# V sums of a block moved ahead of the next K block's last score set, or ahead of its maxima

## The chip, the cores and the metric

The kernel runs on one core of a Trainium2 chip. The metric is the device time of one execution in microseconds. Three executions of the kernel before took 405.64, 403.96 and 405.98 us; the median is 405.64 us.

## The reference

One token of decoding. The input row is normalised, and then an attention block over a cached context and a mixer MLP are both applied to the normalised row and added to it. Cut to what matters:

```python
# x: 1 x 1024 (bf16), 32 query heads, 4 KV heads, 65536 cached keys, head size 128
xn = layernorm(x)
q = (xn @ wq)                                     # 32 heads of 128
scores = einsum("bhqd,bhkd->bhqk", q, k) * (128 ** -0.5)   # 8 query heads share one KV head
o = einsum("bhqk,bhkd->bhqd", softmax(scores), v)
attention = o @ wo
h = gelu(layernorm(xn) @ w1)
x1 = xn + shifted(h) @ w2      # S = 1: the shift along the sequence brings in zeros
mlp = x1 + gelu(layernorm(x1) @ w3) @ w4
out = xn + attention + mlp
```

The K and V caches are 4 x 65536 x 128 bf16 each, 67 MB apiece. With the weights, 169.87 MB are read from HBM in each execution.

## The kernel before, in words

**Blocks and slots.** Each KV head's cache is cut into two blocks of 32768 keys. There are eight K blocks, K0 to K7, and eight V blocks, V0 to V7; each is one transfer of 128 partitions x 32768 bf16, 8.39 MB. On-chip memory has room for three such tiles, `slot0`, `slot1` and `slot2`. The table `home` (lines 285 to 288) says who lives where: even K blocks in slot 0, odd K blocks in slot 2, V0 to V6 in slot 1, V7 in slot 0. The weights pass through the same slots: wq in 0, w3 and later wo in 1, w1 and w2 and later w4 in 2.

**Transfers.** All large loads are issued by SP, one after the other, in the order in which they are recorded: wq, w3, w1 and w2, K0, K1, V0, K2, and then by the list `stream` (line 524): after the V sums of block u come V(u+1) and K(u+3); after block 5 come V6 and V7, after block 6 wo and w4 in five pieces. A load waits on SP until the readers of its slot are done; what is queued behind it waits too.

**The recorder.** Nothing is emitted directly. A `Program` records every operation with the regions of memory that it reads and writes, in the order of the Python code. `plan` (line 124) then goes through the list and gives each operation the waits that this order implies: an operation that reads or writes a region waits for the earlier operations that wrote it, and one that writes a region also for the earlier ones that read it. Each engine executes its operations in the recorded order. In the profile almost all operations therefore have one of the recorder's lines (82, 89, 102, 106, 116, 122), and they are told apart by their tiles.

**One block u.** `scores(u)` (line 453) handles the K block in four sets (`SETS`), each a quarter of every partition's words. For a set, DVE transposes the quarter in place (tile `slot`), and PE then runs 16 matmuls of it against the placed queries (`qdiag`) into `sc`. All 64 matmuls of a block accumulate into the same four PSUM banks. `maxima(u)` (line 469) takes the maximum of `sc` on DVE into `mx`, turns it with a small PE matmul into `pm`, reduces and scales it there, turns it back, and copies it to `nball`. `weights(u)` (line 480) makes `p_sb` with one Exp on ACT, and DVE transposes `p_sb`. `values(u, after)` (line 486) runs 64 matmuls of `p_sb` against the V block into `oacc`, and then records the loads in `after`, here `stream[u]`. `first_rows` copies `oacc` to `og` on ACT after the first block of a head; `group_weights` and `group_rows` bring both blocks of a head together on DVE, with one PE matmul.

**The loop.** Block 0 goes through scores, maxima and weights first. Then for u from 0 to 6 the loop records the scores of block u+1, its maxima, on odd u the group weights, the V sums of block u, the rows, and the weights of block u+1. There is one `p_sb`, so the weights of block u+1 can be written only when the V sums of block u have read theirs.

**The end.** After the last V sums, PE adds o @ wo and the last MLP product as the pieces of wo and w4 land, and the result is stored.

Of the kernel before, what the change touches and what calls it, by code (L numbers as in the profile page):

```python
# [17 lines left out]
SETS = 4  # L18
# [188 lines left out]
def kernel(  # L207
# [83 lines left out]
    def load(it):  # L291
        t = tiles[it]
        if it == "wq":
            prog.load("sp", t[:], A_wq.rearrange("(p c) n -> p (c n)", c=DC))
        elif it == "w3":
            prog.load("sp", t[:, 0:DC * F], B_w3.rearrange("(p c) f -> p (c f)", c=DC))
        elif it == "w12":
            prog.load("sp", t[:, 0:DC * D], B_w1.rearrange("(p c) n -> p (c n)", c=DC))
            prog.load("sp", t[:, DC * D:2 * DC * D], B_w2.rearrange("(m c) n -> m (c n)", c=DC))
        elif it == "wo":  # L300
            prog.load("sp", t[:], A_wo.rearrange("(p j) n -> p (j n)", p=P))
        elif it == "w4":
            w4_v = B_w4.rearrange("(m c) n -> m c n", c=FC)
            c0 = 0
            for n in W4_PIECES:
                prog.load("sp", t[:, c0 * D:(c0 + n) * D], w4_v[:, c0:c0 + n, :].rearrange("p c n -> p (c n)"))
                c0 += n
        else:
            kind, i = it
            g, b = divmod(i, NB)  # L310
            cache = A_k_cache if kind == "K" else A_v_cache
            prog.load("sp", t[:], cache[0, g, b * UKEYS:(b + 1) * UKEYS, :].rearrange("(p ct) d -> p (ct d)", p=P))
# [96 lines left out]
    def place_queries(g):  # L409
        for a in range(4):  # L410
            at = slice(32 * a, 32 * a + 32)
            pool.tensor_copy(
                out=qdiag[at, LEAD:].rearrange("p (x c) -> p x c", x=4)[:, :, 32 * a:32 * a + 8],
                in_=qx[at, :, 8 * g:8 * g + 8])
# [35 lines left out]
    rl = sb("rl", [P, 1])  # L450
    o5 = sb("o5", [P, 32])

    def scores(u):
        g, b = divmod(u, NB)
        if b == 0:
            place_queries(g)
        t = tiles["K", u]
        cols = t[:].rearrange("p (s u k b x r) -> p s u k b x r", u=SUBS, s=SETS, k=16, b=2, r=2)
        for s in range(SETS):
            words = t[:, W * s:W * (s + 1)].bitcast(F32)  # L460
            dve.transpose(out=words, in_=words)
            for b2 in range(2):
                for r in range(2):
                    c0 = LEAD + P * (2 * b2 + r) - 8 * s
                    for e in range(SUBS):
                        pe.mm(sc[:, e, :], qdiag[:, c0:c0 + P], cols[:, s, e, :, b2, :, r],
                              s == 0 and b2 == 0 and r == 0, s == SETS - 1 and b2 == 1 and r == 1)

    def maxima(u):
        g, b = divmod(u, NB)  # L470
        dve.reduce_max(out=mx[:], in_=sc[:].rearrange("p e n -> p (e n)"), axis=AX.X)
        at = next_pm()
        pe.turn32(at[0:1, 0:P], mx[:, 0:1], ident_f[:])
        dve.tensor_reduce(out=m8[:], in_=at[0:1, 0:P].rearrange("o (j h) -> o h j", h=8), axis=AX.X, op=ALU.max)
        dve.tensor_scalar(out=rep[:].rearrange("o (j h) -> o j h", h=8),
                          in0=m8[:].unsqueeze(1).to_broadcast([1, P // 8, 8]), scalar1=-SCALE, scalar2=None, op0=ALU.mult)
        pe.turn32(at[:, P:P + 1], rep[0:1, :], ident_f[0:1, 0:1])
        dve.tensor_copy(out=nball[g % 2][:, b:b + 1], in_=at[:, P:P + 1])

    def weights(u):  # L480
        g, b = divmod(u, NB)
        act.activation(out=p_sb[:], in_=sc[:].rearrange("p e n -> p (e n)"), func=ACTF.Exp,
                       bias=nball[g % 2][:, b:b + 1], scale=SCALE, accum_out=lall[g % 2][:, b:b + 1])
        dve.transpose(out=p_sb[:], in_=p_sb[:])

    def values(u, after):
        vt = tiles["V", u][:].rearrange("p (s u t d) -> p s u t d", u=SUBS, s=SETS, t=16)
        for e in range(SUBS):
            for t in range(16):
                q = t % 4  # L490
                pe.mm(oacc[32 * q:32 * (q + 1), :], p_sb[:, 512 * e + 32 * t:512 * e + 32 * (t + 1)],
                      vt[:, :, e, t, :], e == 0 and t < 4, e == SUBS - 1 and t >= 12, (0, 32 * q), COLS)
        for it in after:
            load(it)

    def first_rows():
        act.copy(out=og[:], in_=oacc[:])

    def group_weights(g):
        dve.tensor_reduce(out=negmg[:], in_=nball[g % 2][:], axis=AX.X, op=ALU.min)  # L500
        act.activation(out=wb[:], in_=nball[g % 2][:], func=ACTF.Exp, bias=negmg[:, 0:1], scale=-1.0)
        dve.tensor_scalar(out=og[:], in0=og[:], scalar1=wb[:, 0:1], scalar2=None, op0=ALU.mult)
        dve.tensor_tensor_reduce(out=lw[:], in0=lall[g % 2][:], in1=wb[:], scale=1.0, scalar=0.0,
                                 op0=ALU.mult, op1=ALU.add, accum_out=ol[:, DH:DH + 1])

    def group_rows(g):
        at = next_pm()
        dve.scalar_tensor_tensor(out=og[:], in0=oacc[:], scalar=wb[:, 1:2], in1=og[:], op0=ALU.mult, op1=ALU.add)
        own = og[:].rearrange("p (s d) -> p s d", d=DH)
        dve.tensor_tensor(out=own, in0=own, in1=mask4[:].unsqueeze(2).to_broadcast([P, 4, DH]), op=ALU.mult)  # L510
        dve.tensor_reduce(out=ol[:, 0:DH], in_=og[:].rearrange("p (s d) -> p d s", d=DH), axis=AX.X, op=ALU.add)
        pe.mm32(at[:, 0:DH + 1], selx[:], ol[:], True, True)
        mine = slice(32 * g, 32 * g + 32)
        dve.reciprocal(out=rl[mine, :], in_=at[mine, P:P + 1])
        dve.tensor_tensor(out=msk[mine, :].rearrange("p (q j) -> p q j", q=4),
                          in0=at[mine, 0:P].rearrange("p (q j) -> p q j", q=4),
                          in1=maskq[mine, :].unsqueeze(2).to_broadcast([32, 4, 32]), op=ALU.mult)
        dve.tensor_reduce(out=o5[mine, :], in_=msk[mine, :].rearrange("p (q j) -> p j q", q=4), axis=AX.X, op=ALU.add)
        dve.tensor_scalar(out=oT[mine, :], in0=o5[mine, :], scalar1=rl[mine, 0:1], scalar2=None, op0=ALU.mult)
# [3 lines left out]
    compute_w12()  # L523
    stream = [[("V", u + 1), ("K", u + 3)] for u in range(NU - 3)] + [[("V", NU - 2), ("V", NU - 1)], ["wo", "w4"]]
    scores(0)
    load(("K", 2))
    maxima(0)
    weights(0)
    for u in range(NU - 1):
        g, b = divmod(u, NB)  # L530
        scores(u + 1)
        maxima(u + 1)
        if b == 1:
            group_weights(g)
        values(u, stream[u])
        if b == 0:
            first_rows()
        else:
            group_rows(g)
        weights(u + 1)  # L540
# [81 lines left out]
```

## Time and profile before

| What | Value |
|---|---|
| median of 3 runs | 405.64 us (403.96 to 405.98) |
| profiled execution, its own time | 404.04 us |
| its span, first to last instruction | 402.6 us |
| mean granted TensorE clock | 0.792 |
| PE busy | 221.1 us (55%) |
| DVE busy | 209.9 us (52%) |
| ACT busy | 27.2 us (7%) |
| HBM read | 169.87 MB, mean 422 GB/s over the span |
| SP's transfers | 98.1% of 16 engines' span |

How to read the rows that follow: times are microseconds from the first instruction. "PE", "DVE", "ACT" and "POOL" are TensorE, VectorE, ScalarE and GpSimd; "SPq" is a transfer's issue on SyncE, not its duration. "slot<-slot" is DVE's transpose of a quarter of a K block, "sc<-slot,qdiag" a score matmul, "oacc<-slot,p_sb" a matmul of the V sums. PEclk is the TensorE clock that was granted, as a share of full speed. The DMA share is the mean busy share of the core's 16 DMA engines.

### The profile page before, as it was taken

To read this page: it belongs to the slowest core of one execution; us is meant where nothing else is said; L and a number is where in the kernel's file an instruction comes from. 1 tells how busy PE (TensorE), PEld (TensorE's weight loads), DVE (VectorE), ACT (ScalarE), POOL (GpSimd) and SP (SyncE) were. 2 spreads that over 40 slices of the span, in tenths; PEclk is the share of its full clock that TensorE was granted. 3 is DMA by queue.
4 is the path that set the end of the run, shared out by engine and by line. 5 is a ranking of instruction groups with operands and counts; after the bars stand their busy time and mean duration, and the time that the engine had idled before them with its cause. 6 is when DMAs were issued, how large, how long until landed. Compare 5 with 4: busy or idle time off the path is not lost.

```text
span 402.6 us, 2557 instructions
## 1 busy us (share of the span) xinstructions
PE 221.1 (55%) x1360; PEld 46.2 (11%) x890; DVE 209.9 (52%) x156; ACT 27.2 (7%) x35; POOL 6.2 (2%) x29
## 2 busy tenths in 40 slices
PE   0250970591794497369607850976096329625096
PEld 0210010000001012101200020002011101112043
DVE  0520010966963983696249647950795669322101
ACT  1010030002002000200020020002000200020000
POOL 2000000000000000000000000000000000000000
PEclk9996896696699597659667985696589859987579
DMA  9989999999997999999999999999999999999995
GB/s 365 462 371 430 457 417 449 463 430 423 423 417 314 417 469 464 417 417 417 425 417 443 482 412 417 423 430 417 488 425 417 423 430 423 484 423 418 394 440 242
DMA packets 3760, 170.03 MB, mean 422 GB/s; under 512 B 419, under 2 KB 421, under 8 KB 678
## 3 DMA queue, kind: packets, MB, share of 16 engines
q1 hardware_dynamic: 3744, 169.87, 98.1%
q8 instruction: 9, 0.15, 0.1%
q14 instruction: 1, 0.01, 0.0%
q10 hardware_dynamic: 6, 0.00, 0.0%
HBM read 169.87 MB, written 0.00 MB: 422 GB/s over the span
## 4 chain that ended last, share of the span: by engine, by line
DMA 49%; PE 25%; DVE 23%; ACT 1%; SPq 1%; issue 1%
DMA slot<-in_A_k_cache_dram 33%; PE sc L106 16%; DVE slot L82 16%; DMA slot<-in_B_w_dram 11%; PE oacc L106 7%; DMA slot<-in_A_wq_dram 5%; DVE mx L82 3%; DVE p_sb L82 2%; ACT p_sb L82 1%; PE pm L122 1%; SPq L89 1%; DVE m L82 0%; DVE og L82 0%; DVE rep L82 0%; DVE ol L82 0%
## 5 line engine op out<-in xcount | busy, mean ns | idle before, releaser
L106 PE MATMUL sc<-slot,qdiag 128*128 128x512 bf16 x512 | 130.7, 417 | 91.2 <-DVE slot L82 91.0
L82 DVE STREAM_TRANSPOSE slot<-slot 128x4096 f32<-128x4096 f32 x32 | 139.2, 4408 | 27.1 <-DMA slot<-in_A_k_cache_dram 27.1
L82 DVE STREAM_TRANSPOSE p_sb<-p_sb 128x2048 bf16<-128x2048 bf16 (+2 forms) x10 | 20.8, 2083 | 55.9 <-ACT p_sb L82 55.7
L106 PE MATMUL oacc<-slot,p_sb 128*32 128x512 bf16 x512 | 42.5, 506 | 8.9 <-DMA slot<-in_A_v_cache_dram 8.9
L102 PEld LDWEIGHTS <-qdiag 128*128 128x128 bf16 x128 | 13.3, 104 | 204.1 <-issue 204.1
L82 DVE TENSOR_REDUCE mx<-sc 128x1 f32<-128x2048 f32 x8 | 18.3, 2292 | 30.1 <-PE sc L106 30.1
L106 PE MATMUL sc<-slot,ln_rep_b 128*32 128x512 bf16 (+1 forms) x80 | 16.3, 834 | 9.7 <-DMA slot<-in_B_w_dram 9.5
L102 PEld LDWEIGHTS <-p_sb 128*32 128x32 bf16 x512 | 16.6, 123 | 31.5 <-issue 20.6
L82 ACT ACTIVATE p_sb<-sc,nball 128x2048 bf16<-128x2048 f32 x8 | 15.8, 1970 | 49.6 <-DVE nball L82 36.0
L106 PE MATMUL psB<-slot,oT 128*32 128x512 bf16 x64 | 9.3, 461 | 11.0 <-DMA slot<-in_A_wo_dram 11.0
L82 DVE SCALAR_TENSOR_TENSOR og<-oacc,wb,og 128x512 f32<-128x512 f32 x4 | 3.0, 751 | 20.1 <-PE oacc L106 20.1
L82 DVE TENSOR_TENSOR og<-psB,slot 64x512 f32<-64x512 f32 x1 | 0.7, 684 | 24.2 <-PE psB L106 24.2
L122 PE MATMUL pm<-ident_f,mx 128*1 128x128 f32 x8 | 2.4, 295 | 19.1 <-DVE mx L82 19.1
L82 ACT COPY og<-oacc 128x512 f32<-128x512 f32 x4 | 2.3, 586 | 142.8 <-PE oacc L106 142.8
L116 PE MATMUL pm<-ol,selx 128*128 128x129 f32 x8 | 2.6, 414 | 10.6 <-DVE ol L82 10.6
L116 PE MATMUL pm<-ln_rowsum_a,msk 128*128 128x1 f32 x2 | 0.6, 363 | 13.4 <-DVE ln_rowsum_a L82 13.4
L106 PE MATMUL sc<-slot,ln_rep_a 128*32 128x512 bf16 x64 | 5.1, 488 | 4.7 <-DMA slot<-in_A_wq_dram 4.7
L82 POOL COPY qdiag<-qx 32x32 bf16<-32x32 bf16 x16 | 3.2, 203 | 261.5 <-PE sc L106 235.4
L82 ACT ACTIVATE wb<-nball,negmg 128x2 f32<-128x2 f32 x4 | 1.2, 296 | 89.6 <-DVE negmg L82 89.6
L82 DVE STREAM_TRANSPOSE p_sb<-x_row 32x256 bf16<-32x256 bf16 x4 | 2.5, 616 | 7.5 <-DMA x_row<-in_A_x_dram 7.5
L102 PEld LDWEIGHTS <-oT 128*32 128x32 bf16 x64 | 4.2, 113 | 15.7 <-issue 12.3
L106 PE MATMUL psB<-slot,hT 128*32 128x512 bf16 x40 | 4.7, 379 | 1.2 <-DMA slot<-in_B_w_dram 1.2
(86 smaller groups left out, 61.2 us busy)
## 6 DMA issues: line engine op xcount, KB each, us to landing
slot<-in_B_w_dram SPq DMA_DIRECT2D x1, 7168.0 KB, 37.7
slot<-in_B_w_dram SPq DMA_DIRECT2D x3, 2048.0 KB, 43.2
slot<-in_B_w_dram SPq DMA_DIRECT2D x1, 3072.0 KB, 39.5
slot<-in_B_w_dram SPq DMA_DIRECT2D x1, 1280.0 KB, 42.1
slot<-in_B_w_dram SPq DMA_DIRECT2D x1, 512.0 KB, 42.9
slot<-in_B_w_dram SPq DMA_DIRECT2D x1, 256.0 KB, 43.0
slot<-in_A_k_cache_dram SPq DMA_DIRECT2D x8, 43.6
slot<-in_A_v_cache_dram SPq DMA_DIRECT2D x8, 27.8
```

The costliest lines, as they stand in the source:

```text
L82: return program.add(Op(engine, lambda: method(*args, **kw), reads, writes, alone=kw.get("accum_out") is not None))
L89: return self.add(Op(engine, lambda: e.dma_start(out=out, in_=in_), [], [out], transfer=True))
L102: self.add(Op("pe", lambda: pe.ldweights(lhsT, tile_position=pos), [lhsT], []))
L106: return pe.add_instruction(mybir.InstMatmult(name=nc.get_next_instruction_name(), engine=mybir.EngineType.PE, start_tensor_calc=start, st ...
L116: return self.add(Op("pe", lambda: pe.matmul(out, lhsT=lhsT, rhs=rhs, start=start, stop=stop, tile_position=pos, skip_group_check=True), [ ...
L122: return self.add(Op("pe", lambda: pe.transpose(out, in_, identity), [in_, identity], [out]))
```

## The change

The function `scores` takes a callable, `before_last`, and runs it ahead of its last set. For u = 0 the loop passes in the V sums of block 0 with their loads; they are then recorded between the third and the fourth set of block 1. For u from 1 to 6 the V sums with their loads are recorded after the scores of block u+1 and ahead of its maxima. All other steps keep their order. The number of instructions on each engine stays the same.

```diff
-    def scores(u):
+    def scores(u, before_last=lambda: None):
         g, b = divmod(u, NB)
         if b == 0:
             place_queries(g)
         t = tiles["K", u]
         cols = t[:].rearrange("p (s u k b x r) -> p s u k b x r", u=SUBS, s=SETS, k=16, b=2, r=2)
         for s in range(SETS):
+            if s == SETS - 1:
+                before_last()
             words = t[:, W * s:W * (s + 1)].bitcast(F32)
             dve.transpose(out=words, in_=words)
...
     for u in range(NU - 1):
         g, b = divmod(u, NB)
-        scores(u + 1)
+        if u == 0:
+            scores(1, lambda: values(0, stream[0]))
+        else:
+            scores(u + 1)
+            values(u, stream[u])
         maxima(u + 1)
         if b == 1:
             group_weights(g)
-        values(u, stream[u])
         if b == 0:
             first_rows()
         else:
```

## The prediction

> **What bounds the kernel now.** I read the page first, its slices above all, then the stretches by time, the issues on SP's queue, and the chain of waits.
>
> The slices of the page (busy tenths of the DMA engines, GB/s):
>
> ```profile
> span 402.6 us, 2557 instructions
> DMA  9989999999997999999999999999999999999995
> GB/s 365 462 371 430 457 417 449 463 430 423 423 417 314 417 469 464 417 417 417 425 417 443 482 412 417 423 430 417 488 425 417 423 430 423 484 423 418 394 440 242
> ```
>
> The transfers fill the whole span but for one slice, the thirteenth (120.8 to 130.8 us): 7 tenths, 314 GB/s. By stretches (the last two columns are DMA share and GB/s, the one before them PE's clock):
>
> ```profile
> 110.00:120.00 10.00, 9.71 (x46) 0.96 (x10) 6.57 (x2) 0.00 (x0) 0.00 (x0) 1.00 0.98 426
> 120.00:131.00 11.00, 4.31 (x68) 1.91 (x67) 4.00 (x5) 2.55 (x3) 0.81 (x4) 1.00 0.74 293
> 131.00:170.00 39.00, 24.50 (x132) 4.67 (x84) 27.70 (x22) 2.35 (x3) 0.00 (x0) 0.73 1.00 431
> 170.00:209.00 39.00, 23.53 (x130) 4.20 (x82) 22.68 (x11) 2.55 (x3) 0.81 (x4) 0.72 1.01 431
> ```
>
> Outside 120 to 131 us the DMA engines are full at about 431 GB/s while PE and DVE each idle for over a quarter of the time. SP's issues say why the hole is there:
>
> ```profile
> 91.13 0.33 SPq L89 DMA_DIRECT2D slot<-in_A_k_cache_dram  x1
> 127.36 0.33 SPq L89 DMA_DIRECT2D slot<-in_A_v_cache_dram  x1
> 127.73 0.43 SPq L89 DMA_DIRECT2D slot<-in_A_k_cache_dram  x1
> 163.39 0.33 SPq L89 DMA_DIRECT2D slot<-in_A_v_cache_dram  x1
> ```
>
> K2 goes out at 91.13, and nothing more until V1 at 127.36, when V block 0's sums free slot 1. From the chain of waits, the K blocks whose landing DVE awaits (start, us, what):
>
> ```profile
> 28.21 41.77 DMA slot<-in_A_k_cache_dram
> ...
> 201.38 46.44 DMA slot<-in_A_k_cache_dram
> 247.82 0.02 issue
> 247.84 4.46 DVE slot L82
> 252.30 0.04 issue
> 252.34 16.91 PE sc L106 x64
> ...
> 279.68 45.63 DMA slot<-in_A_k_cache_dram
> ```
>
> K0 lands at 69.98 (28.21 + 41.77), K5 at 247.82, K7 at 325.31. Between K5 and K7 lie four loads of 8.39 MB in 77.49 us: 19.4 us each, 38.8 a pair, 432 GB/s. K4 lands at 208.92 by the timeline (DVE idles 3.02 us for it). So from K4 on everything is paced by a queue that never empties: what shifts a landing shifts the end by as much, and compute saved there gains nothing.
>
> **The change, part by part.** *Blocks 1 to 6: V sums ahead of the maxima.* PE then goes from scores to V sums without the 3.4 us in which it waits for the maxima (153.37 to 156.99), and V(u+1) and K(u+3) are issued earlier. In the block before, the V sums took 6.39 us at clock 0.50 (156.99 to 163.38) after that wait, and 3.60 in block 0 (123.74 to 127.34), where the clock had stayed at 1.00. DVE's maximum (2.30 us) comes to lie beside the V sums. Gain about 3 to 6 us a block, all hidden: V2 was issued at 163.4 with K3 still landing until about 170, V3 at 201.0 with K4 landing at 208.9. Price in the end: 0.
>
> The Trainium skill (TensorE: Matmul & The Clock Gate, Part 1) speaks for this part: PE is halved after an idle window of about 3.4 us, so closing the wait keeps it at full clock. If PE were the bound, that would be some 2.8 us in each block that now runs cold; by the rows here PE is not, so I count nothing.
>
> *Block 0: V sums ahead of the last score set of block 1.* Sets 0 to 2 of block 1 end on PE by 116.4 (set 3 starts at 116.62). V sums of 3.6 us then end at 120.0, and V1 is issued there, 7.4 us earlier and before K2's stream ends. The hole closes. Its size: K3 lands now at 208.92 - 38.8 = 170.1; without a hole at 69.98 + 5 x 19.4 = 167.0. That is 3.1 us.
>
> *But `values(0, stream[0])` issues two loads, and the second is K3.* K3 belongs in slot 2, and so does K1, whose last quarter has not been transposed or read when `before_last` runs. The recorder orders by what is recorded first: K3's load writes all of slot 2, so DVE's transpose of the last quarter, recorded after it, must wait for K3's landing. In the built instruction order DVE's fourth slot transpose of block 1 has a landing wait of its own, which it has not now (and the set is computed on K3's words). The wait is on the path: behind it stand PE's last 16 score matmuls, and by the in-order queues all of K2's scores, block 1's V sums and, on SP, V2 and K4, which need those V sums. After K3 nothing is queued, so the DMA engines run dry. Working from K3's landing at 167.0:
>
> - transpose of the quarter: 4.5 (row 247.84)
> - 16 score matmuls from a cold PE: 6.2. Warm they take 3.63 (row 116.62). In block 3's first set, started cold at 174.42, weight loads come every 1.71 us and the fifth at 180.24, so that the set ends near 180.6. Bounds 3.6 and 4 x 1.71 = 6.9; the nearest row is the cold start.
> - maximum 2.3; two PE turns, two small DVE operations and the copy 1.4 (122.59 to 123.94); hand-offs 0.1
> - Exp with its accumulator read 2.1 (94.86 to 96.93); transpose of p 2.3
> - scores of K2, landed long ago: 21.1 from DVE's first transpose to PE's last matmul (132.25 to 153.37; other blocks 21.0 to 21.4)
> - V sums of block 1: 3.6, straight after 16 us of matmuls at full clock; bounds 3.6 and 6.5 (cold blocks)
>
> Sum 43.6: V2 and K4 are issued at 210.6. To land both from an empty queue: V1 at 127.36 to K3 at 170.1 took 42.7; wq with nothing ahead took 22.1, so 22.1 + 19.4 = 41.5 bounds it below. With 42.7 K4 lands at 253.3, in place of 208.92: 44.4 later, the closed hole already in it.
>
> The Trainium skill (DMA: Bandwidth & Descriptors, Anatomy of one DMA) fits a DMA, on the GpSimd path, as 2.0 us fixed plus its bytes at 436 GB/s: 40.5 us for the two, an estimate, and a shift of 42.2. The row is this very pair of transfers, so I keep 42.7.
>
> *Is it made up, or does a second hole follow?* After 210.6: block 2's maxima end 1.4 later (the reduction lies beside the V sums), group weights 1.0, group rows 4.4, transpose of p 2.3, scores 21.1, V sums 3.6: V3 and K5 go out near 244.4. K4 is in flight until 253.3. The hole of today came from an issue 0.8 us ahead of K2's landing (69.98 + 3 x 19.4 = 128.2) and lost 3.1, so an issue should be about 4 us ahead: 8.9 leaves some 5 to spare. From K4 on the order of today returns, limited by transfers. 99.6 MB, V2 to w4, remain at the old rate, so nothing is won back. The tail after the last w4 piece (landed 400.52, end 402.6) is unchanged.
>
> So span 402.6 + 44.4 = 447.0. The profiled execution took 404.04, 1.44 over its span: 448.4. The median, 405.64, is 1.6 above it: 450.0. I take the middle, 449.2.
>
> **Rivals.**
> - *The last quarter does not wait for K3* (faster; the change does only what it is called). The hole closes and the rest stays: 405.64 - 3.1 = 402.5. It decides if DVE's fourth transpose starts near 112 us as now. For it: in today's trace no set after a block's first waits for a transfer. Against: the overlap in slot 2 and the order of recording leave no other wait. 3%.
> - *The wait is half as long.* Were K3 fetched ahead of V1, it would land near 147.6, V2 go out near 191.2, K4 land at 233.9: about +25, 430. Against: SP issues V first (127.36, then 127.73), and wq landed in 22.1 us although w3 and w12 were queued at 2.31, so loads of one queue are served one after the other. 2%.
> - *A second hole or a cold clock on the path.* V sums of block 1 at half clock add 2.8, and each microsecond past the spare 5 before V3 adds one: 452 to 455. For it: five of the seven V sums of the loop run partly or wholly cold today. Against: all of them come after PE's 3.4 us wait, which is gone. 8%.
>
> **How the numbers follow.** The forecast has 86%, the rivals 3, 2 and 8, and 1% is left for no net change. Low end: a warm set 3 (-2.6) or the quick restart (-1.2) on 448.4, hardly both: 445.5. High end: the cold V sums (+2.8) or set 3 at 6.9 (+0.7) on 450.0: 453.5. That takes in about half of the third rival. A measurement here can tell about 0.5%, 2 us (the three runs spread over 2.0). Faster 0.03, same 0.01, slower 0.96.
>
> **What would show it.** Right: V1 and K3 issued near 120.0 and 120.4; no hole near 126; DVE idle from about 112 to 167 until K3's landing, PE from 120 to 171; V2 issued near 210.6; DMA slices near zero from 168 to 211 and full afterwards; K4 awaited until about 253; V sums of blocks 1 to 6 near 3.6 us. Wrong: DVE's fourth transpose of block 1 before 120, or V2 issued before 190; then the wait on K3 is not what I take it for. A K4 landing of 253 with an end past 455 would show a second hole.

## The result and the profile after

The changed kernel takes 447.51 us (median of 4 runs, 447.48 to 447.65), the kernel before 405.54 (4 runs, 403.96 to 405.98). The ratio is 1.1043, with a 95% interval of 1.1013 to 1.1073. The profiled execution took 447.53 us, its span is 445.9.

The slices of the page after (busy tenths of the DMA engines, GB/s; a slice is now 11.1 us):

```profile
span 445.9 us, 2554 instructions
DMA  9999999999999960002898998999989999999996
GB/s 376 443 427 389 441 459 459 394 459 406 442 464 394 459 294 0 0 0 90 382 470 388 454 459 388 466 411 435 470 388 460 423 423 464 394 448 441 419 411 260
```

The small hole of the thirteenth slice is gone. From the fifteenth slice on the transfers die down, three slices are empty, and in the nineteenth they come back. By stretches (the last three columns are PE's clock, the DMA share and GB/s):

```profile
120.00:131.00 11.00, 0.00 (x0) 0.00 (x0) 0.00 (x0) 0.56 (x1) 0.00 (x0) 0.70 0.96 417
131.00:170.00 39.00, 0.00 (x0) 0.00 (x0) 2.97 (x1) 0.00 (x0) 0.00 (x0) 0.50 0.85 368
170.00:209.00 39.00, 24.69 (x134) 3.62 (x77) 26.32 (x11) 2.06 (x2) 0.81 (x4) 0.80 0.00 0
209.00:248.00 39.00, 22.13 (x151) 4.39 (x95) 28.50 (x24) 4.88 (x6) 0.81 (x4) 0.82 0.98 417
```

From 120 to 131 us the engines now run at 417 GB/s, where they had 293. From 131 to 167 PE and DVE stand still while the transfers run; from 170 to 209 the transfers stand still while PE and DVE work. What lay side by side before lies one behind the other. The timeline shows the wait (in brackets: how long the engine idled, and for what):

```profile
116.29 3.64 PE L106 MATMUL oacc<-slot,p_sb 128*32 128x512 bf16 x64
119.97 0.33 SPq L89 DMA_DIRECT2D slot<-in_A_v_cache_dram  x1
120.34 0.43 SPq L89 DMA_DIRECT2D slot<-in_A_k_cache_dram  x1
167.03 4.45 DVE L82 STREAM_TRANSPOSE slot<-slot 128x4096 f32<-128x4096 f32 x1 [54.35 <-DMA slot<-in_A_k_cache_dram]
171.53 5.66 PE L106 MATMUL sc<-slot,qdiag 128*128 128x512 bf16 x16 [51.60 <-DVE slot L82]
...
206.23 3.64 PE L106 MATMUL oacc<-slot,p_sb 128*32 128x512 bf16 x64
209.91 0.33 SPq L89 DMA_DIRECT2D slot<-in_A_v_cache_dram  x1
```

DVE waits 54.35 us for K3 before it may transpose the last quarter of block 1. K3 was issued at 120.34, V2 not before 209.91. K4 then lands at 252.62, and V3 goes out ahead of that:

```profile
243.28 0.33 SPq L89 DMA_DIRECT2D slot<-in_A_v_cache_dram  x1
252.64 17.42 DVE L82 STREAM_TRANSPOSE slot<-slot 128x4096 f32<-128x4096 f32 x4 [3.74 <-DMA slot<-in_A_k_cache_dram]
```

The order of recording also changes what is computed. K3's load overwrites the last quarter of K1 before any engine has read it, so the kernel after leaves those keys out: it scores a quarter of K3 in their place, and block 3 later transposes that quarter a second time.

### The profile page after: what moved, and what is told of

The parts are those of the page before. It is cut to its first block, busy times and chain, and to the rows that moved or that the text cites. A ratio compares the mean times of both kernels' runs of the same rounds, so it can differ in the third digit from the quotient of the medians.

```text
span 445.9 us, 2554 instructions
## 1 busy us (share of the span) xinstructions
PE 209.0 (47%) x1360; PEld 43.0 (10%) x890; DVE 209.9 (47%) x156; ACT 27.3 (6%) x35; POOL 6.2 (1%) x29
## 4 chain that ended last, share of the span: by engine, by line
DMA 46%; DVE 26%; PE 22%; another core or an unknown queue 3%; ACT 2%; SPq 1%; issue 1%
DMA slot<-in_A_k_cache_dram 31%; DVE slot L82 20%; PE sc L106 16%; DMA slot<-in_B_w_dram 11%; DMA slot<-in_A_wq_dram 5%; PE oacc L106 5%; DVE p_sb L82 3%; ACT p_sb L82 1%; DVE mx L82 1%; DVE og L82 1%; PE pm L122 1%; SPq L89 1%; DVE ol L82 0%; DVE m L82 0%
## 5 line engine op out<-in xcount | busy, mean ns | idle before, releaser
L106 PE MATMUL oacc<-slot,p_sb 128*32 128x512 bf16 x512 | 30.9, 397 | 13.0 <-DMA slot<-in_A_v_cache_dram 13.0
L102 PEld LDWEIGHTS <-p_sb 128*32 128x32 bf16 x512 | 13.6, 100 | 34.0 <-issue 17.9
L82 DVE TENSOR_REDUCE m<-pm 1x8 f32<-1x128 f32 x8 | 2.2, 279 | 9.7 <-PE pm L122 9.7
```

Source lines behind the costliest of these rows:

```text
L82: return program.add(Op(engine, lambda: method(*args, **kw), reads, writes, alone=kw.get("accum_out") is not None))
L102: self.add(Op("pe", lambda: pe.ldweights(lhsT, tile_position=pos), [lhsT], []))
L106: return pe.add_instruction(mybir.InstMatmult(name=nc.get_next_instruction_name(), engine=mybir.EngineType.PE, start_tensor_calc=start, st ...
```

## The experiments

Every time is a median, and the brackets hold the lowest and the highest run. Every ratio is to runs of the kernel before on the same chip, with its 95% interval; it lies near the quotient of the mean times, not of the medians. Every profile is of a single execution.

### Only K3's load moved behind the set

```diff
-            scores(1, lambda: values(0, stream[0]))
+            scores(1, lambda: values(0, stream[0][:1]))
+            load(stream[0][1])
```

> The change with one load moved: V sums of block 0 and V1's load stay ahead of block 1's last set, K3's load is recorded after that set. My theory (the whole loss is the last set's wait for K3's landing, and the change is otherwise a small gain): DVE's fourth transpose starts near 112 us, V1 goes out near 120.0, K3 near 123.7, the hole at 126 us is gone, and the time is 405.5 - 3.1 = 402.4 us. Rival (the V sums between sets 3 and 4 of a block, or ahead of the maxima, cost time by themselves, and K3 is only a part of it): slower than 405.5.

Measured: 400.86 us (400.63 to 401.76) against 406.37; ratio 0.9879 (0.9844 to 0.9914). From the timeline, block 0's V sums, block 1's last set and the issues:

```profile
116.50 3.64 PE L106 MATMUL oacc<-slot,p_sb 128*32 128x512 bf16 x64
120.07 3.64 PE L106 MATMUL sc<-slot,qdiag 128*128 128x512 bf16 x16
120.18 0.33 SPq L89 DMA_DIRECT2D slot<-in_A_v_cache_dram  x1
...
123.74 0.33 SPq L89 DMA_DIRECT2D slot<-in_A_k_cache_dram  x1
```

The V sums stand where the change put them, and the set follows at once. One load's place in the record is the whole of the loss: 46.6 us between two kernels whose code differs in nothing else (here the set is again computed on K1's words). The rival (V sums inside the scores cost by themselves) falls. The gain against the kernel before is 5.5 us by the medians, more than the 3.1 expected; the runs below say why.

### K3 ahead of V1

```diff
-            scores(1, lambda: values(0, stream[0]))
+            scores(1, lambda: values(0, stream[0][::-1]))
```

> The change with the two early loads swapped: K3 goes out ahead of V1 (block 1's last set is computed on K3's words, as in the change). My theory (the set waits for K3's landing, and loads of SP's queue are served one after the other): K3 lands one load earlier, near 147.6 in place of 167.0, V2 goes out near 190.5 in place of 209.9, and the time is 19.4 us less than the change's 447.5, that is 428. Rival (the wait is for the whole queue, or the two loads share the engines): 447 to 448, K3 landing near 167.

Measured: 428.47 us (427.58 to 428.68); ratio 1.0543 (1.0526 to 1.0561). K3's landing ends DVE's wait at 147.65, V2 goes out at 190.8, K4's landing ends DVE's next wait for a transfer at 233.51:

```profile
147.65 4.45 DVE L82 STREAM_TRANSPOSE slot<-slot 128x4096 f32<-128x4096 f32 x1 [35.30 <-DMA slot<-in_A_k_cache_dram]
233.51 17.42 DVE L82 STREAM_TRANSPOSE slot<-slot 128x4096 f32<-128x4096 f32 x4 [3.73 <-DMA slot<-in_A_k_cache_dram]
```

19.0 us come back, one load's 19.4 within half a microsecond. The set waits for K3, not for the queue, and loads of one queue are served in turn.

### Only the first part of the change

Blocks 1 to 6 go back to the order of before:

```diff
         if u == 0:
             scores(1, lambda: values(0, stream[0]))
         else:
             scores(u + 1)
-            values(u, stream[u])
         maxima(u + 1)
         if b == 1:
             group_weights(g)
+        if u > 0:
+            values(u, stream[u])
```

> Only the first part of the change: V sums of block 0 with both loads ahead of block 1's last set, which is then computed on K3's words as in the change; blocks 1 to 6 in the order of the kernel before. My theory: after K3 the queue is empty, so PE's order in block 1 is on the path there: the maximum (2.3) and its turns (1.4) stand ahead of block 1's V sums, and these may run at half clock (3.6 to 6.4 us). V2 goes out 3.7 to 6.5 us after 209.9, and the time is 451 to 454 us. Rival (the second part of the change is worth nothing anywhere): 447.5.

Measured: 453.16 us (453.05 to 454.41); ratio 1.1172 (1.1123 to 1.1221). Block 1's V sums and V2's issue:

```profile
209.96 6.56 PE L106 MATMUL oacc<-slot,p_sb 128*32 128x512 bf16 x64
216.57 0.33 SPq L89 DMA_DIRECT2D slot<-in_A_v_cache_dram  x1
```

V2 goes out 6.7 us later than in the change, of which 0.5 is K3's later landing (167.56 in place of 167.03). The profiled execution is the longest of the four, 6.9 us over the change's; the medians differ by 5.7. While the queue is empty PE's order is on the path, and the second part of the change earns those microseconds there.

### Only the second part of the change

```diff
-        if u == 0:
-            scores(1, lambda: values(0, stream[0]))
-        else:
-            scores(u + 1)
+        scores(u + 1)
+        if u > 0:
             values(u, stream[u])
         maxima(u + 1)
+        if u == 0:
+            values(0, stream[0])
```

> Only the second part of the change: block 0 goes as in the kernel before, blocks 1 to 6 have their V sums ahead of the maxima. My theory (this part is hidden, because the transfer queue never empties there): V2 goes out some 6 us earlier than 163.4, V sums of blocks 1 to 6 take about 3.6 us, and the time is that of the kernel before, 405.5 within 1 us. Rival (PE's order is on the path in these blocks): 3 us or more faster, up to 6 x 3 = 18.

Measured: 405.42 us (403.84 to 406.74, 12 runs) against 406.37; ratio 0.9987 (0.9961 to 1.0013). The V sums of blocks 1 to 6 take 3.64 us each, V3 goes out at 197.74 in place of 201.01, and no gain clear of noise comes of it. Hidden, as forecast. V2 goes out at 159.96, only 3.4 us earlier than in the kernel before and not 6, since block 0's V sums ended 3.1 us later. They ran at another clock here than in the profile of before:

```profile
123.98 6.42 PE L106 MATMUL oacc<-slot,p_sb 128*32 128x512 bf16 x64
130.46 0.33 SPq L89 DMA_DIRECT2D slot<-in_A_v_cache_dram  x1
```

The stretch from 126 to 130 us, first in the profile of before, then in this one (the last three columns are PE's clock, the DMA share and GB/s):

```profile
126.00:130.00 4.00, 1.31 (x28) 0.52 (x17) 0.06 (x1) 2.55 (x3) 0.00 (x0) 1.00 0.80 266
126.00:130.00 4.00, 4.00 (x44) 1.53 (x40) 0.00 (x0) 0.00 (x0) 0.00 (x0) 0.54 0.02 4
```

PE's wait for the maxima ahead of these V sums is nearly the same (3.4 and 3.6 us, with two small matmuls in it), but here the granted clock fell to 0.54 and they took 6.42 us in place of 3.64. V1 went out 3.1 us later, and the span is 405.2 in place of 402.6. The Trainium skill (TensorE: Matmul & The Clock Gate, Part 1) says that the clock follows an activity window of about 3.4 us that runs freely, so that the point at which it changes depends on where in the window the work falls. That a pause about as long as the window halves the clock in one execution and not in another would follow from it; these two profiles agree.

### The wait filled with matmuls

On the kernel before:

```diff
         at = next_pm()
+        if u == 1:
+            other = pm[1 - nb_pm[0]]
+            for n in range(10):
+                pe.mm(other[:], qdiag[:, LEAD:LEAD + P], tiles["K", u][:, 512 * n:512 * (n + 1)], n == 0, n == 9)
         pe.turn32(at[0:1, 0:P], mx[:, 0:1], ident_f[:])
```

> The kernel before with ten extra matmuls of 512 columns (a result that nobody reads) on PE while it waits for block 1's maximum; nothing else is changed. It asks what spreads the kernel before over 403.5 to 407.8 us. My theory: the V sums of block 0 run at full or at half clock (3.6 us in the profile of before, 6.4 in that with block 0 as before), which moves V1's issue and so the hole by 2.8 us. With PE kept busy they take 3.6 us always, and all runs lie within 403.4 to 404.5. Rival (the spread is from the transfers themselves): the runs spread over 3 us or more as before.

Measured: 403.91 us (403.50 to 404.95, 6 runs) against 406.25 (405.29 to 407.05, 11 runs); ratio 0.9944 (0.9929 to 0.9958). Ten useless matmuls save 2.3 us. The V sums ran at full clock in its profile:

```profile
123.95 3.64 PE L106 MATMUL oacc<-slot,p_sb 128*32 128x512 bf16 x64
127.64 0.33 SPq L89 DMA_DIRECT2D slot<-in_A_v_cache_dram  x1
```

Its longest run, 404.95, is shorter than the shortest of its neighbours, 405.29, though 0.45 above my bound. So the time of the kernel before depends on whether PE is busy in one pause. By the spans with K3's load moved (399.3), before (402.6) and block 0 as before (405.2), the hole costs 3.3 us with full-clock V sums and 5.9 with half-clock ones. The V sums of other blocks in the profile of before also take 5.3 us, and the 21 runs of the kernel before on the chip of the run with K3's load moved lie in three groups: 403.5 to 403.9 (6 runs), 405.5 to 405.8 (4) and 406.4 to 407.8 (11). No run of the kernel before with slow V sums in block 0 was profiled, so that these groups are the clock's is argued from the two other kernels, not shown.

### All blocks alike, V sums behind the whole score set

```diff
-        if u == 0:
-            scores(1, lambda: values(0, stream[0]))
-        else:
-            scores(u + 1)
-            values(u, stream[u])
+        scores(u + 1)
+        values(u, stream[u])
         maxima(u + 1)
```

> All seven blocks alike, V sums after the whole of the next block's scores and ahead of its maxima. V1 goes out near 123.9, about 4.2 us ahead of K2's landing at about 128.1 (the kernel before: 0.8 us ahead, a hole of 3.1 us). My theory (an issue about 4 us ahead of the last queued landing leaves no hole): 402.4 us, the same as with K3's load after the set. Rival (the queue needs a longer lead, 8 us as with V1 at 120.0): between 402.4 and 405.5.

Measured: 402.37 us (401.74 to 403.96); ratio 0.9919 (0.9891 to 0.9946). V1 goes out at 124.07. The number is the one expected, but its reason is not: the run with K3's load moved, which should have been equal, takes 1.5 us less. The stretch from 120 to 131 us has 389 GB/s here and 423 there (second line):

```profile
120.00:131.00 11.00, 4.44 (x69) 1.91 (x67) 6.56 (x6) 2.65 (x3) 0.82 (x4) 0.91 0.96 389
120.00:131.00 11.00, 4.20 (x22) 0.69 (x7) 4.42 (x5) 2.65 (x3) 0.82 (x4) 0.91 0.98 423
```

A lead of 4 us does not close the hole altogether. How the loss reaches the end is not shown: DVE's wait for K3 ends only 0.2 us later here (167.53 in place of 167.31), that for K4 1.1 us later (207.15 in place of 206.02).

### V1's issue held back by one matmul

```diff
-            scores(1, lambda: values(0, stream[0][:1]))
-            load(stream[0][1])
+            scores(1, lambda: values(0, [], 0, 63))
+            values(0, stream[0], 63, 64)
```

The two new arguments of `values` are the first matmul of its 64 that it runs and the one ahead of which it stops.

> As the run with K3's load moved (400.9 us), but the last of block 0's 64 V matmuls stands behind block 1's last set, and both loads follow it: PE's work is the same within 0.3 us, and V1 goes out near 124.0 in place of 120.2, as in the run with all blocks ahead of their maxima (402.4 us). If V1's later issue is what those 1.5 us are (a lead of 4.5 us ahead of K2's landing does not close the hole fully): about 402.4. If they come from PE's order (V sums behind the whole score set): 400.9.

Measured: 401.79 us (401.35 to 404.20), V1 at 123.66; ratio 0.9914 (0.9882 to 0.9945). The stretch from 120 to 131 us:

```profile
120.00:131.00 11.00, 4.11 (x19) 0.69 (x7) 4.83 (x5) 2.65 (x3) 0.82 (x4) 0.82 0.94 399
```

Beside it the kernel above once more:

> All seven blocks with V sums behind the next block's scores and ahead of its maxima, run beside the one above on one chip. 402.4 again, V1 near 124.1.

Measured: 402.68 us (401.28 to 402.99), V1 at 124.19; ratio 0.9919 (0.9892 to 0.9946). Holding V1 back costs 0.9 us with the same work on PE and takes the transfer rate of that stretch from 423 to 399 GB/s, so the lead counts. The 0.9 us are a comparison across two chips, on which the kernel above took 402.37 and 402.68, and the two ratios overlap; the rates are of one execution each. The other 0.9 us between the two kernels here (389 GB/s in the repeat too) may be the half microsecond of lead between them or PE's order. That is left open.

### V sums one set earlier still

```diff
-            if s == SETS - 1:
+            if s == SETS - 2:
                 before_last()
```

on the run with K3's load moved.

> V sums of block 0 and V1's load one set earlier still, ahead of block 1's third set; K3's load after the fourth set, as in the run with K3's load moved. My theory (the hole is closed once V1 goes out some 4 us ahead of K2's landing, and the transfers bound the rest): V1 near 116, the time the same as that run's, 400.9 within 0.6 us. Rival (there was still some of the hole left): 0.7 us or more faster.

Measured: 400.73 us (400.58 to 400.89), V1 at 117.11, a microsecond later than expected; ratio 0.9865 (0.9850 to 0.9879). No more comes of a still earlier issue. The table orders the spans by the lead of V1's issue ahead of K2's landing. That landing, 128.5, is an estimate: K3's landing with K3's load moved, less a pair, 167.31 - 38.8. By the way of the prediction (69.98 + 3 x 19.4 = 128.2) every lead is 0.3 us shorter.

| V1 issued at | lead, us | span, us | kernel |
|---|---|---|---|
| 117.11 | 11.4 | 399.4 | one set earlier |
| 120.18 | 8.3 | 399.3 | K3's load moved |
| 123.66 | 4.8 | 399.9 | one matmul behind |
| 124.07, 124.19 | 4.4, 4.3 | 400.9, 401.1 | all blocks alike |
| 127.36 | 1.1 | 402.6 | before, V sums at full clock |
| 130.46 | -2.0 | 405.2 | block 0 as before, V sums at half clock |

Each span is of one execution. The kernels of the first two rows take less time than the kernel before, by 1.35 and 1.2%, and by their intervals that is clear of noise.

## Why the prediction was right

The forecast was 449.2 us, measured are 447.5. Its steps:

| Step | predicted | measured |
|---|---|---|
| V1 and K3 issued | 120.0, 120.4 | 119.97, 120.34 |
| K3 lands, the small hole closed | 167.0 | 167.00 |
| quarter's transpose | 4.5 | 4.46 |
| 16 score matmuls, cold PE | 6.2 (3.6 to 6.9) | 5.67 |
| maximum, turns and hand-offs | 3.8 | 3.7 |
| Exp and transpose of p | 4.4 | 4.4 |
| scores of K2 | 21.1 | 21.0 |
| V sums of block 1 | 3.6 (3.6 to 6.5) | 3.57 |
| V2 issued | 210.6 | 209.91 |
| from that issue to K4's landing | 42.7 (from 41.5) | 42.7 |
| K4 lands | 253.3 | 252.6 |
| V3 issued, ahead of K4's landing | 244.4, by 8.9 | 243.28, by 9.3 |
| span | 447.0 | 445.9 |

The measured column is from the chain of waits of the profile after, whose lines from the stall on read (start, us, what):

```profile
120.34 46.66 DMA slot<-in_A_k_cache_dram
167.00 0.02 issue
167.03 4.46 DVE slot L82
171.48 0.04 issue
171.53 5.67 PE sc L106 x16
...
202.67 3.63 PE sc L106 x16
206.30 3.57 PE oacc L106 x64
```

The mechanism is the one forecast, and the first two experiments show it rather than argue it: with K3's load behind the set the loss is gone, and with K3 one load earlier one load's time comes back. The terms that were off:

- The cold set took 5.67 us, 0.5 less than the row I took; the granted clock was 0.50 up to 175.0 us and 0.84 from there to 177.2, so it came back some 4 us after the set's start at 171.53. In the row that I took (set start 174.42, clock 0.50 up to 178 us and 0.72 from there to 181) it came back some 5 us after the start. That is most of the 0.7 by which V2 is early. From K4's landing to the end it is 193.3 us, 193.7 before, which is the rest of the span's error.
- The step from the profile to the median was wrong in kind. I put the forecast between 448.4, from the profiled execution, and 450.0, from the median. The filled wait points to what lies between those two: the hole of before, which is larger in most executions than in the profiled one (2.3 us were saved there). The change closes that hole whatever its size: its four runs lie within 0.2 us of each other, those of before within 2.0. So the shift is to be added to the profiled execution: 448.4 is 0.9 above the measured time, 450.0 is 2.5 above it. With the measured spans the sum is 404.04 + (445.9 - 402.6) = 447.3.
- The hole's 3.1 us was right for the profiled execution (402.6 - 399.3 = 3.3, with K3's load moved) and too small for the median (5.5).
- That an issue about 4 us ahead leaves no hole was wrong; at 4.3 to 4.8 us the span is still 0.6 to 1.8 us over the best. It did no harm, since V3 went out 9.3 us ahead of K4's landing.
- Three small readings were off, and the result hangs on none of them: from 153.37 to 156.99 is 3.6 us and not 3.4, 4 x 1.71 is 6.8 and not 6.9, and the mean clock over the V sums near 157 us is 0.56 and not 0.50.

Of the rivals, the first (no wait for K3) falls with DVE's 54.35 us. The second (K3 fetched first) is not what the change does, but built as a kernel of its own it gave 428.5 where the rival said 430. The third (cold V sums, a second hole) did not come: all V sums of blocks 0 to 6 took 3.64 us, and K5 landed 38.7 us after K4.

The price of the restart, 42.7 us from an issue into an empty queue to the second landing, came out to a tenth. It was taken from the row of the hole, where by the prediction's own sum the queue still had 0.8 us of K2 left, so it was a neighbour's price and not quite this one. The runs bear it out: from V's issue to K's landing took 42.7 us here, 42.7 with K3 ahead of V1 (190.78 to 233.49), and 42.5 with block 0 as before (130.46 to 173.00).

The estimate by the fit that the Trainium skill gives for the GpSimd path (DMA: Bandwidth & Descriptors, Anatomy of one DMA) would have been 2.2 us short, so here the row decides.

## What to carry to other kernels

Where a recorder derives the waits from the order of the code, a load moved up is a write moved up: list who still reads its slot, for they will wait for the new data (and compute on it). On a kernel bound by transfers, look for the queue's holes and ask of each edit only when the next load is issued and whether anything is left in the queue by then; here time saved on the engines behind a full queue was worth nothing that could be measured (405.42 against 406.37 us), while with the queue empty an issue 6.7 us later made the time 5.7 us longer. Add a shift to the profiled execution rather than to a median of runs that differ in the very term that the edit removes.

## What the runs showed of the hardware

A pause of about 3.5 us on PE left the clock at full speed in one execution (1.00 from 126 to 130 us) and about halved it in another (0.54), and with it the 64 V matmuls behind it took 3.64 or 6.42 us; ten useless matmuls in the pause took 2.3 us off the time. A queue that was filled again some 4.3 to 4.8 us ahead of its last landing still lost 0.6 to 1.8 us of span in single executions (0.9 to 1.8 by the medians); with 8.3 us of lead it lost no more than with 11.4. Loads of one queue were served in turn: issued ahead of V1 and not behind it, K3 landed at 147.65 in place of 167.03.
